# The opening of a fused light-convolution and max-of-three feed-forward kernel: how its weights arrive and are split, how the first tap sums are turned, and the order of its first steps

## The chip, the cores and the metric

One core of one Trainium2 chip runs the whole program. The metric is the device time of one execution in microseconds (us), the median of several runs. The profile is one more execution, recorded by the hardware.

## The reference, cut to what matters

```python
w = exp(weight_gen - max over the 7 taps); w = w / (sum over the 7 taps + 1e-9)   # (8, 4160, 8 heads, 7)
x_unf = x_pad[:, arange(S)[:, None] + arange(7)[None, :]]                         # the 7 last tokens
a = einsum('bshk,bskhg->bshg', w, x_unf)          # causal light convolution -> 33280 tokens x 192
h = maximum(maximum(a @ w1, a @ w2), a @ w3)      # w1, w2, w3: 192 x 768
out = h @ w_out                                   # w_out: 768 x 192
```

`x` and `weight_gen` are float32. The four weight matrices are float64, so each weight comes in as two 32-bit words.

## The kernel before

The 33280 tokens are cut into 65 chunks of 512 (`CH`), four token tiles of 128 each (`TC`). For a chunk, `taps` makes one product per tile (7 taps side by side, 1344 columns, line 492) on GpSimd or VectorE and sums it over the taps (line 504 on VectorE). The sum is turned so that its 192 features lie on the partitions: 128 of them in one tile (`xa`), the last 64 (`DB`) in another (`xc`). `up` multiplies by the differences w2-w1 and w3-w1 and takes maxima with zero; the part of w1 goes through a 192x192 matrix w1 @ w_out that `compose` builds once. `down` multiplies by w_out. So that the result is exact enough, every operand is a rounded high part and a low rest (`xa_hi`, `xa_lo`; `wa_hi`, `wa_lo`; `xc`, `xb`; `wb_hi`, `wb_lo`), and products are taken high by high, high by low and low by high.

Each product uses 64 rows of the TensorE array: the lower half of the rows ("L") and the upper half ("U") work on different products at the same time, but never in one bank together (`products`, line 1081). A bank is begun by L, then SyncE passes the word on, then U finishes it. So U trails L by some products, and all instructions of both stand in one TensorE queue in a fixed order. There are 8 PSUM banks (`"bank": 8`). One group `up c, j` is two banks with 18 products, 9 on each half of the rows. The weights of the last 64 features (`wb`) are kept on both halves of the partitions; block j of 128 columns of the feed-forward layer has its low rest (`wb_lo`) on the half `odd` only. Before, `jp, odd = divmod(j, 2)`, so every second block has five products on L and four on U, the others four and five.

The order on each engine is made by the program itself: `Plan` holds tasks with a cost, a due time and the buffers that they hold, and lays them out by a list schedule. The order of the first two chunks (`c < ON_TENSOR`) and of all weight preparation is written out by hand in `OPENING` (line 271). The steps there: `load*` issue DMAs on SyncE; `softmax` s; `singles` turns float64 into float32 (`single`, line 723); `a`, `b` are the weight differences (by two products with the identity and its negative on TensorE, lines 855 and 861, or on GpSimd, line 840); `rests` the low rests (line 902 on VectorE or GpSimd); `warm` n runs n products of the identity with itself (line 800); `turn x` and `turn y` turn the token sums (lines 538, 545, 557, 558); `turn` j turns w1 (lines 1013, 1014); `parts` makes high and low tokens (lines 611 to 634); `up`, `compose`, `down` as above. Everything whole (all 128 rows) on TensorE waits for the last U product before it.

In `single`, before, ScalarE takes the absolute value of the high word (line 742), VectorE or GpSimd clamps it (line 759; or ScalarE by two more passes, line 752), VectorE shifts (766), puts in the sign (775) and the top bits of the low word (784). The six loads of the last 64 rows (`load_b`, line 699) bring pieces of 1 KB, each load to 64 partitions (192 KB).

Of the kernel before, what the change touches and what calls it, by code (L numbers as in the profile page):

```python
# [12 lines left out]
U32 = mybir.dt.uint32  # L13
AF = mybir.ActivationFunctionType
# [179 lines left out]
def lightconv_maxout_kernel(  # L194
# [44 lines left out]
    CLAMP_ON_POOL = (("a", 0, 0), ("a", 2, 1), ("b", 2), ("d", 0), ("d", 1), ("d", 2),)  # L239
    CLAMP_ON_SCALAR = (("a", 1, 0), ("a", 2, 0), ("b", 1),)  # L240
    LOAD_DUE = {
        ("s", 0): -57,
        ("a", 0): -65,
        ("b",): -36,
        ("s", 1): -44,
        ("a", 1): -21,
        ("a", 2): -54,
        ("d",): 4,
# [9 lines left out]
    for c in range(1, NC):  # L258
# [7 lines left out]
    F_MAX = float(np.array(0x47EFFFFF, np.uint32).view(np.float32))  # L266
    F_MIN = float(np.array(0x38000000, np.uint32).view(np.float32))
# [6 lines left out]
        ("singles", 2), ("singles down",), ("taps", 0), ("taps", 1), ("warm", 27), ("a", 0, 1, 2),  # L274
        ("a", 0, 0, 1), ("turn x", 0, 1), ("turn x", 0, 0), ("turn x", 0, 2), ("turn y", 0, 1),
        ("turn x", 0, 3), ("turn", 5), ("turn y", 0, 2), ("turn", 0), ("turn", 1), ("a", 2, 0, 2),
# [3 lines left out]
        ("rests", "b", 0), ("parts", 0), ("turn y", 1, 3), ("turn", 4), ("b", 2),  # L280
# [10 lines left out]
    wb_hi = const.tile([P, NJ, NI, P], F32R, name="wb_hi")  # L291
# [28 lines left out]
        "bhi": ([P, NI, P], F32R),  # L320
# [5 lines left out]
        "bhi": 2, "raw": 1,  # L326
# [53 lines left out]
    def load_super(s):  # L380
# [14 lines left out]
        w = transfer(0.07 * n, weights, (), due, [hw])  # L395
# [127 lines left out]
    def turn_tokens(c, t):  # L523

        ha, sums = tapped[c]
        got, ba, bb = turned[c]
        to = slice(t * P, (t + 1) * P)

        if (c, t) in SUMS_ON_TENSOR:
            p, hr = sums[t]  # L530

            hb, hs = hold("bank"), hold("ob")

            def total():

                for k in range(K):
                    pin(
                        nc.tensor.matmul(
                            buf(hb)[:, :D], ident, buf(hr)[:, k], start=k == 0, stop=k == K - 1
                        )  # L540
                    )

            summed = whole(2.35, total, [p], [hb, hr])
            out = plan.add(
                "ACT", act(D), lambda: pin(nc.scalar.copy(buf(hs), buf(hb)[:, :D])), [summed],
                None, [hb, hs],
            )
            later["x", c, t] = [(hs, out)]
            return
        turn_sum(c, t, sums[t], lambda: buf(ha)[:, t], ha)  # L550
# [15 lines left out]
    def opening_parts(c):  # L566
        for t in range(TC):
            turn_later(c, t)
# [758 lines left out]
```

## Time and profile before

| | |
|---|---|
| median of 3 runs | 1409.42 us (1407.21 to 1411.99) |
| the profiled execution | 1407.7 us, of which its span is 1405.9 us |
| TensorE matmul busy | 1395.5 us, 99% of the span |
| VectorE, ScalarE, GpSimd busy | 72%, 80%, 78% |
| first product of an `up` | 36.0 us into the span |

Start by asking when the main products begin and whether they ever stop after that; then look at each engine in the stage before they begin. The busy share of TensorE counts pipelined products and also the identity products of `warm`, so it is no measure of progress in the opening.

### The profile page before, as it was taken

The page shows a single profiled execution, that of the slowest core. Times are in us where ns is not written, and L with a number is a line of the kernel's source. Part 1 is how long each engine was busy: PE and PEld are TensorE (multiplying, and loading weights), DVE is VectorE, ACT ScalarE, POOL GpSimd, SP SyncE. Part 2 cuts the span into 40 slices and gives each one's busy share as a digit, 9 for nine tenths or more (in the row PEclk, how much of TensorE's full clock was granted, in tenths as well). Part 3 has the DMA queues.
Part 4 walks back from the last instruction along what each step waited for, and adds up shares of the span by engine and source line. Part 5 has one row for each costly group of instructions (what it writes and reads, how often), then busy time and mean ns, then how long its engine had stood idle before and what let it go on. Part 6 is the DMA issues. An engine that isn't in the chain of part 4 may idle for free.

```text
span 1405.9 us, 37245 instructions
## 1 busy us (share of the span) xinstructions
PE 1395.5 (99%) x15000; PEld 1325.8 (94%) x15000; DVE 1009.6 (72%) x1378; ACT 1124.5 (80%) x2871; POOL 1095.1 (78%) x604
## 2 busy tenths in 40 slices
PE   8999999999999999999999999999999999999999
PEld 6999999999999999999999999999999999999998
DVE  7978777676687677677677677668668767767543
ACT  5787888887887787788788788788788778778873
POOL 6999898877887877887787788787788787788321
PEclk9999999999999999999999999999999999999999
DMA  7121111110111111111111011111011111110000
GB/s 257 47 70 70 59 70 70 59 70 24 59 70 69 59 70 37 57 59 69 70 58 63 31 59 69 70 59 69 24 59 70 70 59 70 35 55 15 24 24 23
DMA packets 23004, 85.10 MB, mean 61 GB/s; under 512 B 2488, under 2 KB 9144, under 8 KB 18864
## 3 DMA queue, kind: packets, MB, share of 16 engines
q1 hardware_dynamic: 22832, 82.73, 16.1%
q8 instruction: 117, 1.92, 0.6%
q14 instruction: 55, 0.45, 0.1%
HBM read 57.16 MB, written 25.56 MB: 59 GB/s over the span
## 4 chain that ended last, share of the span: by engine, by line
PE 98%; DMA 1%; SPq 0%; ACT 0%; DVE 0%; issue 0%
PE bank L1091 97%; DMA h_lo<-in_moe_w_dram 1%; DMA room<-in_moe_w_out_dram 0%; PE bank L1031 0%; SPq L683 0%; PE bank L861 0%; PE bank L855 0%; SPq L385 0%; PE bank L1014 0%; ACT xc L616 0%; PE bank L1013 0%; DVE bank L775 0%; PE bank L557 0%; SPq L390 0%; ACT wb_hi L967 0%
## 5 line engine op out<-in xcount | busy, mean ns | idle before, releaser
L492 POOL TENSOR_TENSOR r<-xt,wt 128x1344 f32<-128x1344 f32 x257 | 720.1, 2859 | 153.8 <-DVE acc L504 151.2
L1091 PE MATMUL bank<-wo,h_hi 64*128 64x384 f32 x3120 | 659.6, 355 | 0.0
L1091 PE MATMUL bank<-wo,h_lo 64*128 64x192 f32 x3120 | 593.2, 247 | 0.0
L1091 PE MATMUL bank<-xa_hi,wa_hi 64*128 64x512 f32 x1560 | 503.5, 389 | 0.0
L1091 PE MATMUL bank<-xa_lo,wa_hi 64*128 64x512 f32 x1560 | 500.2, 387 | 0.0
L1091 PE MATMUL bank<-xa_hi,wa_lo 64*128 64x512 f32 x1560 | 499.9, 387 | 0.0
L599 ACT COPY room<-room 32x128 f32<-32x128 f32 x1512 | 448.8, 297 | 63.7 <-DVE room L588 41.0
L1091 PEld LDWEIGHTS bank<-wo,h_lo 64*128 64x128 f32 x3120 | 486.2, 187 | 0.0
L1091 PEld LDWEIGHTS bank<-wo,h_hi 64*128 64x128 f32 x3120 | 482.6, 185 | 0.0
L504 DVE TENSOR_REDUCE acc<-r 128x192 f32<-128x1344 f32 x256 | 394.6, 1541 | 6.1 <-POOL r L492 5.6
L1091 PE MATMUL bank<-xc,wb_hi 64*128 64x512 f32 x780 | 293.4, 386 | 0.0
L1091 PE MATMUL bank<-xb,wb_hi 64*128 64x512 f32 x780 | 279.2, 387 | 0.0
L1091 PE MATMUL bank<-xc,wb_lo 64*128 64x512 f32 x780 | 278.4, 386 | 0.0
L1091 PEld LDWEIGHTS bank<-xa_lo,wa_hi 64*128 64x128 f32 x1560 | 265.6, 184 | 13.4
L1091 PEld LDWEIGHTS bank<-xa_hi,wa_lo 64*128 64x128 f32 x1560 | 265.2, 184 | 13.4 <-POOL wa_lo L902 0.2
L1148 ACT ACTIVATE m<-bank 128x512 f32<-128x512 f32 x390 | 233.1, 598 | 52.3 <-PE bank L1091 45.7
L1091 PEld LDWEIGHTS bank<-xa_hi,wa_hi 64*128 64x128 f32 x1560 | 262.2, 184 | 12.2 <-DVE acc L504 0.3
L1224 DVE TENSOR_TENSOR o<-bank,ob 128x192 f32<-128x192 f32 x260 | 90.4, 348 | 229.8 <-ACT ob L1217 229.8
L1167 DVE TENSOR_TENSOR h_lo<-bank,h_hi 128x512 fp32r<-128x512 f32 x258 | 176.4, 684 | 69.1 <-ACT h_hi L1160 68.9
L1167 POOL TENSOR_TENSOR h_lo<-m,h_hi 128x512 fp32r<-128x512 f32 x132 | 174.3, 1321 | 41.8 <-ACT h_hi L1160 41.7
L1156 DVE TENSOR_TENSOR bank<-bank,m 128x512 f32<-128x512 f32 x258 | 177.3, 688 | 19.1 <-ACT m L1148 9.0
L1091 PE MATMUL bank<-wca,xa_hi 64*128 64x384 f32 x520 | 182.7, 352 | 0.0
(104 smaller groups left out, 2043.0 us busy)
## 6 DMA issues: line engine op xcount, KB each, us to landing
xt<-in_x_dram SPq DMA_DIRECT2D x31, 1344.0 KB, 5.9
out_dram<-o SPq DMA_DIRECT2D x64, 384.0 KB, 2.3
wt<-in_weight_gen_dram SPq DMA_DIRECT2D x32, 224.0 KB, 2.5
h_hi<-in_moe_w_dram SPq DMA_DIRECT2D x6, 256.0 KB, 4.6
h_lo<-in_moe_w_dram SPq DMA_DIRECT2D x6, 192.0 KB, 9.8
xt<-in_x_dram SPq DMA_DIRECT2D x1, 960.0 KB, 6.2
raw<-in_moe_w_dram SPq DMA_DIRECT2D x3, 256.0 KB, 6.5
room<-in_moe_w_out_dram SPq DMA_DIRECT2D x2, 384.0 KB, 6.4
```

What stands on the lines that cost most here:

```text
L492: on.tensor_tensor(to, buf(hx)[:, la + t : la + t + K].rearrange("p k (h g) -> p k h g", g=G), wide() .rearrange("p (h k) -> p k h", k=K) ...
L504: pin(nc.vector.tensor_reduce(buf(ha)[:, t], buf(hr), axis=AX.X, op=ALU.add))
L599: pin(nc.scalar.copy(to[:, :, p : p + 32], b[p : p + 32, :, f : f + 32]))
L1091: ins = nc.tensor.matmul(buf(hb)[:, :n], w()[h], v()[h], start=half == 0 and first, stop=half == 1 and last,)
L1148: lambda: pin(nc.scalar.activation(buf(hm), buf(hb), AF.Relu)), [made], due,
L1156: lambda: pin(nc.vector.tensor_tensor(buf(keep), buf(hb), buf(hm), op=ALU.max)),
L1167: eng.tensor_tensor(buf(hl)[:, j], buf(keep), buf(hh)[:, j].bitcast(F32), op=ALU.subtract)
L1224: nc.vector.tensor_tensor(buf(ho)[:, t], buf(hb)[:, :D], buf(hq), op=ALU.add)
```

## The change

The edits, all in the opening but for the last but one:

1. `load_b` reads 3 KB pieces: three neighbouring blocks for one half of the partitions. So `odd, jp = divmod(j, 3)`: blocks 0 to 2 have their own `wb` rows on the lower half, 3 to 5 on the upper half.
2. In the first two chunks `up` uses these rows on their own half alone: the own half makes six products of a bank, the other three. Copies for the other half (`wb_of`) are made after the opening by two ScalarE copies (`change_over`); before, 12 copies (line 967) made both halves at once. For that, the rest of the last 64 features (`xb`) is made on both halves in these chunks.
3. `single`: ScalarE takes the scaled absolute value and, in a second pass over 16-bit words, the top bits of the low word; one minimum on VectorE or GpSimd; two VectorE operations put all together. The ScalarE clamp and the shift of line 766 are gone.
4. The tap sums on TensorE are made by seven transposes that add up in the bank, for each of the two feature parts, straight where they are wanted; before, seven identity products, a ScalarE copy (545) and a transpose. Five tiles instead of four do so; VectorE makes four products instead of three in the opening, all four in the contiguous layout.
5. All `a` and `b` differences and all rests but that of `b` 0 are on GpSimd.
6. `compose` makes its products on the two halves of the rows, without waiting for U.
7. In all chunks, blocks 0 to 2 now have five products on L and four on U, blocks 3 to 5 four and five.
8. `OPENING` is anew: no `warm`, `up 0 0` after c 0's sums and two tiles of c 1; `compose` after three groups instead of eight. Fewer low parts on GpSimd in these chunks (`ON_POOL_FIRST`), new due times of loads (their sequence is as before).

```diff
-    SUMS_ON_TENSOR = ((0, 1), (0, 2), (0, 3), (1, 2),)
+    SUMS_ON_TENSOR = ((0, 0), (0, 1), (0, 3), (1, 0), (1, 1),)
-    ON_POOL_FIRST = (1, 3, 4)
-    TAPS_ON_VECTOR = ((0, 1), (0, 3), (1, 1))
+    ON_POOL_FIRST = (5,)
+    TAPS_ON_VECTOR = ((0, 0), (0, 3), (1, 0), (1, 1))
...
-        ("a", 0): ("L", "DVE"),
+        ("a", 0): ("POOL", "POOL"),
         ("a", 1): ("POOL", "POOL"),
-        ("a", 2): ("L", "DVE"),
-        ("b", 0): ("POOL", "POOL"),
+        ("a", 2): ("POOL", "POOL"),
+        ("b", 0): ("POOL", "L"),
...
+        ("load down",), ("softmax", 0), ("softmax", 1), ("singles", 0), ("singles", 1),
+        ("singles", 2), ("singles down",), ("taps", 0), ("taps", 1), ("turn x", 0, 0),
+        ("turn x", 0, 2), ("a", 0, 1, 2), ("b", 1), ("turn x", 0, 3), ("rests", "b", 1),
+        ("turn x", 0, 1), ("parts", 0), ("turn x", 1, 0), ("b", 2), ("turn x", 1, 1), ("b", 0),
+        ("a", 2, 0, 2), ("turn", 5), ("a", 0, 0, 1), ("up", 0, 0), ("turn", 3), ("turn", 0),
+        ("rests", "b", 0), ("turn x", 1, 2), ("a", 1, 0, 2), ("turn x", 1, 3), ("turn", 4),
+        ("rests", "a", 1), ("turn", 2), ("parts", 1), ("rests", "a", 2), ("turn", 1),
+        ("rests", "a", 0), ("up", 0, 4), ("rests", "b", 2), ("up", 0, 3), ("compose",),
+        ("up", 0, 1), ("up", 0, 2), ("up", 0, 5), ("up", 1, 0), ("up", 1, 5), ("up", 1, 1),
+        ("down", 0), ("up", 1, 4), ("up", 1, 2), ("up", 1, 3),
...
+                for out, f in places():
+                    for k in range(K):
+                        pin(
+                            nc.tensor.matmul(
+                                out, buf(hr)[:, k, f], ident, is_transpose=True, start=k == 0,
+                                stop=k == K - 1,
+                            )
+                        )
...
-                                out=raw_b()[h, :, i].rearrange("p j n w -> p j (n w)"),
-                                in_=w[P:].rearrange("p (j o n) -> p j o n", j=NP, o=2)[:, :, odd],
+                                out=raw_b()[h, i].rearrange("p j n w -> p (j n w)"),
+                                in_=w[P:, odd * NP * 2 * P : (odd + 1) * NP * 2 * P],
...
+                nc.scalar.activation(big(), high().bitcast(F32), AF.Abs, scale=2.0**-112)
+                    fit(), big(), F_MAX, None, op0=ALU.min
+                    word(), source().bitcast(U16)[..., 1], AF.Copy, scale=2.0**-13, bias=-0.4999
...
+            own = half == odd
+            w, by = (wb_hi, [b_hi[jb]]) if own else (wb_of, b_of)
+            if c < ON_TENSOR:
+                got[2:2] = [of_k, of_b] if own else []
+            else:
+                got[2:2] = [of_b if half == low else of_k]
```

## Rows read from the trace of the kernel before

**Rows 1.** Part 4 of the page, by line: the chain of work that ended last, as shares of the span.

```profile
PE bank L1091 97%; DMA h_lo<-in_moe_w_dram 1%; DMA room<-in_moe_w_out_dram 0%; PE bank L1031 0%; SPq L683 0%; PE bank L861 0%; PE bank L855 0%; SPq L385 0%; PE bank L1014 0%; ACT xc L616 0%; PE bank L1013 0%; DVE bank L775 0%; PE bank L557 0%; SPq L390 0%; ACT wb_hi L967 0%
```

**Rows 2.** Busy time by stage: us of the stretch, then busy us (and instructions) of TensorE, its weight loads, VectorE, ScalarE, GpSimd, then TensorE's granted clock, the DMA share and GB/s.

```profile
0.00:36.00 36.00, 29.04 (x157) 24.76 (x157) 27.96 (x44) 19.63 (x50) 22.95 (x24) 0.95 0.76 251
36.00:58.70 22.70, 22.70 (x170) 19.94 (x170) 22.25 (x36) 16.18 (x35) 21.32 (x18) 1.00 0.00 1
...
200.00:400.00 200.00, 200.00 (x2184) 189.34 (x2181) 149.44 (x200) 166.54 (x428) 163.21 (x88) 1.00 0.16 60
```

**Rows 3.** TensorE in order of time, where the first `up` begins and around `compose` (start, us, what). The second row is the first product of U; the two at 54 us are the last of U before `compose`.

```profile
35.99 0.47 PE L1091 MATMUL bank<-xa_hi,wa_hi 64*128 64x512 f32 x1
...
37.48 0.50 PE L1091 MATMUL bank<-xa_hi,wa_hi 64*128 64x512 f32 x1
...
53.91 0.39 PE L1091 MATMUL bank<-xc,wb_hi 64*128 64x512 f32 x1
54.14 0.39 PE L1091 MATMUL bank<-xa_hi,wa_lo 64*128 64x512 f32 x1
54.45 4.31 PE L1031 MATMUL bank<-wo,raw 128*128 128x192 f32 x24
58.70 0.49 PE L1091 MATMUL bank<-xa_hi,wa_hi 64*128 64x512 f32 x1
```

**Rows 4.** The chain of work that ended last, in order of time (start, us, what): one of its pieces ahead of the first `up`, TensorE's products for a difference.

```profile
28.42 1.72 PE bank L861 x4
```

**Rows 5.** Two stretches of the loading, columns as in rows 2, then the packets of two stretches. In 14 to 16 us nearly all are pieces of the 64-partition loads of line 699; in 21.5 to 23.5 us they are pieces of w_out and the last of line 683, to 128 partitions.

```profile
15.00:18.00 3.00, 1.52 (x9) 0.96 (x7) 3.00 (x5) 0.46 (x2) 1.83 (x1) 1.00 1.13 237
...
24.00:27.00 3.00, 1.76 (x9) 1.13 (x10) 3.00 (x5) 2.06 (x7) 3.00 (x3) 1.00 1.07 422
...
DMA packets 447, 0.44 MB, mean 220 GB/s; under 512 B 37, under 2 KB 445, under 8 KB 445
...
DMA packets 512, 0.75 MB, mean 374 GB/s; under 512 B 29, under 2 KB 499, under 8 KB 512
```

**Rows 6.** The float64 split of the last 64 rows and what follows it, in order of time over all engines.

```profile
20.84 0.56 ACT L742 ACTIVATE m<-h_lo 128x384 f32<-128x384 f32 x1 [3.40 <-DMA h_lo<-in_moe_w_dram]
...
24.17 1.01 DVE L784 SCALAR_TENSOR_TENSOR b<-h_lo,bank 128x384 uint32<-128x384 uint32 x2
...
27.00 1.42 POOL L840 TENSOR_TENSOR b<-b 128x256 f32<-128x256 f32 x2
...
27.76 0.41 ACT L949 CAST bhi<-b 128x256 fp32r<-128x256 f32 x1 [0.50 <-POOL b L840]
...
28.38 0.73 POOL L902 TENSOR_TENSOR wb_lo<-b,bhi 128x256 fp32r<-128x256 f32 x1
...
32.12 0.55 DVE L784 SCALAR_TENSOR_TENSOR b<-h_lo,bank 128x384 uint32<-128x384 uint32 x1
```

**Rows 7.** TensorE in order of time: products of `warm` in two short stretches (the first and the second row), the first of eight transposes in a row and the products behind them, then two transposes at 30 us and two at 35 us.

```profile
4.72 1.49 PE L800 MATMUL bank<-ident 128*128 128x128 f32 x6
...
7.79 1.39 PE L800 MATMUL bank<-ident 128*128 128x128 f32 x11
...
25.23 0.33 PE L1013 MATMUL bank<-ident,w1a 128*128 128x128 f32 x1 [1.41 <-DVE b L784]
...
26.86 1.56 PE L855 MATMUL bank<-wx,ident 128*128 128x512 f32 x2
...
29.92 0.42 PE L557 MATMUL bank<-ident,ob 128*128 128x128 f32 x1
30.13 0.42 PE L558 MATMUL bank<-ident,ob 128*64 128x128 f32 x1
...
34.80 0.27 PE L557 MATMUL bank<-ident,acc 128*128 128x128 f32 x1
34.91 0.27 PE L558 MATMUL bank<-ident,acc 128*64 128x128 f32 x1
```

**Rows 8.** The stretch in which TensorE's granted clock was down, columns as in rows 2.

```profile
27.65:31.07 3.42, 3.42 (x10) 2.38 (x10) 3.42 (x6) 2.53 (x6) 2.03 (x4) 0.54 0.14 60
```

**Rows 9.** VectorE in order of time: two tap products in the contiguous layout, and one in the other.

```profile
11.94 3.02 DVE L492 TENSOR_TENSOR r<-xt,bank 128x1344 f32<-128x1344 f32 x2
...
25.57 2.62 DVE L492 TENSOR_TENSOR r<-xt,bank 128x1344 f32<-128x1344 f32 x1
```

**Rows 10.** Groups by line and shape in the first 57 us, of GpSimd and VectorE: count, busy us, mean ns, idle before.

```profile
L492 POOL TENSOR_TENSOR r<-xt,wt 128x1344 f32<-128x1344 f32 x9 | 23.8, 2672 | 3.9 <-PE bank L538 2.4 <-DVE acc L504 1.4
...
L840 POOL TENSOR_TENSOR b<-b 128x256 f32<-128x256 f32 x3 | 2.1, 731 | 0.0
...
L840 POOL TENSOR_TENSOR wx<-wx,w1a 128x512 f32<-128x512 f32 x1 | 1.3, 1287 | 0.0
...
L766 DVE TENSOR_SCALAR bank<-m 128x384 uint32<-128x384 uint32 x4 | 2.1, 548 | 0.0
```

**Rows 11.** TensorE at 311 us: L begins the first `down` of a chunk, and then U the same one.

```profile
311.12 0.33 PE L1091 MATMUL bank<-wca,xa_hi 64*128 64x384 f32 x1
...
313.89 0.33 PE L1091 MATMUL bank<-wca,xa_hi 64*128 64x384 f32 x1
```

**Rows 12.** VectorE at 311 us: the maximum of a block in its bank, and the last reader of that bank.

```profile
311.63 0.69 DVE L1156 TENSOR_TENSOR bank<-bank,m 128x512 f32<-128x512 f32 x1
...
313.45 0.68 DVE L1167 TENSOR_TENSOR h_lo<-bank,h_hi 128x512 fp32r<-128x512 f32 x1
```

More of the change, by code (lines that the diff above doesn't have):

```diff
@@ L527, in turn_tokens @@
         to = slice(t * P, (t + 1) * P)
+        both = c in LAST_ON_TENSOR
+        places = lambda: [
+            (buf(ba)[:, to], slice(0, P)),
+            *([(buf(bb)[:, to], slice(DB, D))] if both else []),
+            (buf(bb)[:DB, to], slice(P, D)),
+        ]
         if (c, t) in SUMS_ON_TENSOR:
             p, hr = sums[t]
[L532 to L539, printed above, removed]
-                        )
-                    )
@@ L543, in turn_tokens @@
[L543 to L548, printed above, removed]
-            return
-        turn_sum(c, t, sums[t], lambda: buf(ha)[:, t], ha)
-    def turn_sum(c, t, made_by, acc, held):
-        got, ba, bb = turned[c]
-        to = slice(t * P, (t + 1) * P)
-        def turn():
-            pin(nc.tensor.transpose(buf(ba)[:, to], acc()[:, :P], ident))
-            pin(nc.tensor.transpose(buf(bb)[:DB, to], acc()[:, P:], ident))
-        got.append(whole(0.36, turn, [made_by], [ba, bb, held]))
@@ L562, in turn_later, with turn @@
-    def turn_later(c, t):
-        for hs, out in later.pop(("x", c, t), ()):
-            turn_sum(c, t, out, lambda: buf(hs), hs)
-    def opening_parts(c):
-        for t in range(TC):
-            turn_later(c, t)
-        got, ba, bb = turned[c]
-        parts(c, [ba, bb], lambda: (buf(ba), buf(bb)[:DB]), got)
+            def turn():
+                for out, f in places():
[5 more added lines that the diff above has]
+                            )
+                        )
@@ L572, in blocks, with turn, opening_parts @@
+            got.append(whole((2.45 if both else 1.65), turn, [p], [ba, bb, hr]))
+            return
+        def turn():
+            for out, f in places():
+                pin(nc.tensor.transpose(out, buf(ha)[:, t, f], ident))
+        got.append(whole(0.47 if both else 0.36, turn, [sums[t]], [ba, bb, ha]))
+    def opening_parts(c):
+        got, ba, bb = turned[c]
+        parts(c, [ba, bb], lambda: (buf(ba), buf(bb) if c in LAST_ON_TENSOR else buf(bb)[:DB]), got)
     def blocks(c, ha, sums):
@@ L618, in parts @@
             )
-            for h in halves
+            for h in to_k
         ]
         for t in cs:
-            t.apart = True
-        name, cost = ("DVE", vec(CH)) if c < ON_TENSOR else ("POOL", gps(CH))
-        eng = nc.vector if c < ON_TENSOR else nc.gpsimd
-        near = halves[0] if c < ON_TENSOR else halves[low]
+            t.apart = len(cs) > 1
+        name, cost = ("DVE", vec(CH)) if first else ("POOL", gps(CH))
+        eng = nc.vector if first else nc.gpsimd
         def a_low():
@@ L1021, in turn_weights, with u_last, after, products @@
         )
+    SLOT = {CH: (0.2275, 0.386), 2 * D: (0.166, 0.358), D: (0.12, 0.247), "c": (0.335, 0.46)}
+    uppers = []
+    last_upper = []
+    def u_last():
+        return last_upper[-1:]
+    def after(ins, other):
+        tc.add_manual_dep(
+            ins.ins,
+            other.ins.name,
+            mybir.DependencyInfo(mybir.DependencyClass.Sync, mybir.DependencyReason.DATA),
+            reason="the two halves of the rows don't write to a bank together",
+        )
+        return ins
+    def products(hb, terms_of, to=None):
+        begun, before, at = {}, [], clock[0]
+        for half in range(2):
+            h = halves[half]
+            terms = terms_of(half)
+            for q, (n, w, v, deps, holds) in enumerate(terms):
+                first, last = q == 0, q == len(terms) - 1
+                def emit(n=n, w=w, v=v, h=h, half=half, first=first, last=last):
+                    ins = nc.tensor.matmul(
+                        to() if to else buf(hb)[:, :n], w()[h], v()[h],
+                        start=half == 0 and first, stop=half == 1 and last,
+                    )
+                    pin(ins)
+                    if half == 0 and last:
+                        begun[0] = pin(after(nc.sync.nop(), ins))
+                    elif half == 1 and first:
+                        after(ins, begun[0])
+                slot, end = SLOT[n]
+                t = plan.add(
+                    "LU"[half], slot, emit, [*deps, *(before if first else [])], at,
+                    [hb, *holds], end=end,
+                )
+                at += slot
+            if half == 0:
+                before = [plan.add("SYNC", 0.0, lambda: None, [t], None, [], end=0.3)]
+            else:
+                last_upper.append(t)
+        return t
     def compose():
```

219 lines of the change are left out of this document (82 added, 137 removed), and 7 rows, old and new, of the table OPENING.

## The prediction

> **What bounds the kernel now.** I read the chain of work that ended last first: the products of line 1091 hold 97% of it [rows 1]. Busy time by stage comes next: from 36 us on TensorE has no idle time and its granted clock is 1.00 [rows 2]. So the time is the moment when the first `up` begins (35.99), plus the products, plus whatever keeps one half of the rows waiting. The reader is to see two such losses in the order of time [rows 3]. U begins 1.49 us after L. And ahead of `compose` L has ended while U goes on: from 35.99 to 58.70 are 22.71 us for eight groups and `compose` (4.25). A product's slot is 0.23 [rows 3]; I use 0.228, so a half's nine slots of a group are 2.05 us and eight groups 16.4. 22.71 - 16.4 - 4.25 leaves 2.06 us lost. The chain ahead of 36 us goes through TensorE's products for a difference [rows 4]; VectorE is busy 27.96 of the first 36 us and 22.25 of the next 22.7 [rows 2], so it is nearly a second bound there.
>
> **Part by part.**
>
> **3 KB pieces.** While the 64-partition loads run, the DMA engines are busy all the time and move 237 GB/s; with 1.5 KB pieces to 128 partitions it is 374, with large ones 422 [rows 5]. The six loads are 1.18 MB: 5.0 us at 237, 3.15 at 374. The gain is 0 to 1.8 us, on the last landing that ScalarE waits for at 20.84 [rows 6]. The rows don't say whether the piece or the 64 partitions limit; 1.5 KB is only half as long again and runs 1.6 times as fast, which a fixed price per piece would hardly give. I take 0 and keep 1.8. The Trainium skill, SBUF — State Buffer, section "Door 1: The DMA port swizzle", speaks against this edit: a transfer to 64 partitions reaches only half of the ports, about 218 GB/s, and two such transfers at once are hardly faster. The trace's 237 agrees; by that rule longer pieces save nothing.
>
> **The split of b.** Before, the three parts are ready at 24.7, 25.2 and 32.7 [rows 6], the last one late by VectorE's queue. New: two ScalarE passes and two VectorE operations of 0.55 for the first part, as the rows of such operations show (0.56 at line 742 [rows 6], 0.548 at line 766 [rows 10]); the minimum is beside the second pass. 20.84 + 4 x 0.55 = 23.0, the others some 1.1 apart. The new 16-bit pass is not in the trace; 0.4 to 0.7 by line 742, 0.55 taken. Then the GpSimd difference (0.73 [rows 10]), ScalarE's copy (0.41 [rows 6]), and on TensorE the rest (768 columns in all, at two records of 0.11 for 128 columns of a plain product [rows 7], 1.3): 25.8 with three hand-overs of 0.1. GpSimd may be in a tap product of 2.67 [rows 10]: half of it on average, so the first `up` begins at 27.1. The other tap sums don't hold it at the full clock: five of 14 transposes at 0.11 [rows 7] are 7.7 us from about 11.6 (the first VectorE product begins at 11.94 now [rows 9] and can begin some 1.9 us earlier, as VectorE has less ahead of it, and takes 1.5).
>
> **From the first `up` to compose.** Group 0,0 has 6 slots on L and 3 on U per bank. L needs 12 slots, and U ends 3 later: 15 x 0.228 = 3.4 us before anything whole may run. Then come five `turn`s (0.41 each: four such pairs stand between 25.23 and 26.86 [rows 7]) and two token turns (0.22 and the gap, 0.36): 2.8 us. Group 0,4 takes 6 slots of L, 1.4. So group 0,3 begins 7.6 us after the first, and its place is 34.7 at the full clock.
>
> **The clock.** After the sums of c 1, TensorE waits for b, as it did at 25 us now. There it had a wait of 1.41 us and eight transposes in a row from 25.23 to 26.86, and the granted clock then was 0.54 in 27.65 to 31.07 [rows 7, 8]. At the 1.2 GHz level a transpose takes 0.21 instead of 0.11 [rows 7]. I expect one such fall around the first `up` and price it by this stretch: 3.4 us in which half the work is done, 1.7 lost. Group 0,3: 36.4, `compose` 1.4 later.
>
> **VectorE and GpSimd to that point.** VectorE: the 30 operations of the split have 11520 columns, 16.4 us at 0.548 for 384 [rows 10]; softmax 2.9, four tap products of 1.5 [rows 9] 6.2 (the third of before took 2.62 in the other layout), three sums 4.6, low parts of c 0 2.1, two groups' maxima and low parts 2.7: 34.9, less 0.09 for each of 48 operations, as neighbours overlap by that much: 30.6 from 4.2. With the 3.6 us of idle time that it has now that is 38.4, against `compose` at 37.8: the two engines meet. GpSimd: four products of 2.67 are 10.7, three `b` and two `a` differences of 0.73 and two of 1.29 are 6.2, and rests of the same lengths 4.8 [rows 6, 10]; softmax 2.5 and minima 2.0: 26.2 from 8.6, 34.8. So even a TensorE without waits would not get group 0,3 before about 34. The dropped identity products of `warm`, ScalarE's 12 copies of `wb` and VectorE's shift lie off this sum: they ran beside it. `change_over` (two ScalarE copies, about 0.75 each) is due 25 us later with ScalarE busy 83% [rows 2]: nothing; if it were late, all of U's products of c 2 wait behind it.
>
> **compose on halves.** 24 records of 4.31 us [rows 3] become 24 of 64 rows on each half, beside each other: the same 4.25. What it saves is the switch, up to the 2.06 us above; I take 2.0, bounds 0 and 2.06.
>
> **Blocks of five and four.** The L and U work of a chunk stays equal. But U trails L by 2.77 us at a chunk's `down`s now [rows 11], which is 12.2 slots; over blocks 3 to 5 L makes 24 products and U 30, so the trail grows to 18.2. At the end of the last chunk the trail is paid: 4 slots more than now, 0.9 us.
>
> **The sum.** By 36.4 L has done 18 slots, 4.1 us of work, which now is done at 35.99 + 4.1 = 40.1: 3.7 us gained. With the switch 2.0 and the trail -0.9: 4.8. The profiled execution's span 1405.9 becomes 1401.1, its own time 1407.7 becomes 1402.9; the median of the runs lies 1.7 above that execution, so 1404.6.
>
> **The rivals.**
>
> **A. Transposes leave the clock down.** Without `warm` TensorE has nothing but transposes until b's rest. In `warm`, plain products were spaced 0.23 at 5 us and 0.11 at 8 us [rows 7], so it starts at the low level. If transposes don't bring it up, each tap sum takes 14 x 0.21 = 2.9: five from 11.6, with a turn, `turn` 5 and the rest of b at half speed (0.4, 0.6, 2.6), end at 29.8. The first `up` loses 1.3 more. Group 0,3 at 38.8; gain 40.1 - 38.8 + 2.0 - 0.9 = 2.4: 1407.0. For: the clock fell behind eight transposes [rows 7, 8]. Against: these stood behind a wait, and were not dense. The Trainium skill, TensorE: Matmul & The Clock Gate, section "Part 4: PE-mode transpose", has this rule: transposes don't count as busy in the same way, and the full clock does not engage for them. The trace's fall agrees but doesn't prove it.
>
> **B. No fall, and b lands sooner.** The first `up` is at 25.3 or before; VectorE then sets `compose`, between 34.8 (no idle time) and 38.4, say 36.5. Group 0,3 at 35.1; gain 6.1, at best 8: 1403.3 to 1401.4. For: 1 KB pieces are the shortest here. Against: the 64 partitions stay.
>
> **C. Banks run out, in every chunk.** With a trail of 18.2 slots and four products to a bank of L, four and a half banks are begun by L and not ended by U, and L is in another; a block's bank is read until 2.5 us behind its maximum [rows 12], two or three more with the first of a pair: 7 to 8 of 8. Where L must wait for a bank, the trail can't grow and then shrink, and the chunk loses that slot on both halves: 0.228 x 63 = 14.4 us for one slot, 1404.6 + 14.4 = 1419. It decides from a third of a slot (4.8 us). Against: half of the blocks give their bank back at the maximum or earlier, and TensorE never waits for a bank now.
>
> **How the numbers follow.** Chances: forecast 0.40 (1402 to 1407.5, by the bounds of GpSimd's wait and of the fall, 0 to 3.4), A 0.30 (1405 to 1411), B 0.18, C 0.12. The range reaches from 1399 to 1412: it leaves out C and a tail of B. 0.3% of this kernel, about what a measurement tells from no change, is 4.2 us, that is 1405.2 below. Faster: B 0.18, half of the forecast 0.22, of A 0.03: 0.43. Slower: C and a tail of A: 0.13. Within: 0.44.
>
> **What would show it.** Right: first `up` near 27, a granted clock near 0.5 around it, `compose` near 38, no idle L ahead of it, 20.8 us a chunk as before. A: transposes of 0.21 up to 29 us. B: ScalarE's wait for b ending by 19.2. C: TensorE waiting for VectorE or ScalarE behind each block 5. Wrong altogether: a product or sum of c 0 late on VectorE or GpSimd, so that the in-order TensorE stands in front of it while others are ready.

## The result, and the profile after

Three rounds on one chip give a median of 1419.97 us for the changed kernel (1418.18 to 1424.81) beside 1409.01 for the kernel before: the ratio is 1.0085 [1.0064, 1.0105]. The change costs 11 us where 4.8 us of gain were forecast, and the time lies outside the range. The profiled execution took 1419.52 us with a span of 1417.6, against a span of 1405.9 before.

The chain that ended last, by line, of the changed kernel (it answers to [rows 1]): the line of the products has moved, and its share has fallen from 97% to 92%.

```profile
PE bank L1041 92%; POOL r L493 3%; DMA h_lo<-in_moe_w_dram 1%; DMA raw<-in_moe_w_dram 0%; POOL h_lo L1162 0%; POOL xb L628 0%; PE bank L544 0%; POOL xa_lo L623 0%; POOL wa_lo L892 0%; SPq L680 0%; POOL wt L457 0%; POOL wt L435 0%; POOL m L746 0%; ACT bank L756 0%; DVE r L493 0%
```

Busy time by stage, of the changed kernel (it answers to [rows 2], same columns and stretches):

```profile
0.00:36.00 36.00, 18.32 (x102) 15.08 (x102) 27.13 (x41) 18.82 (x44) 25.97 (x27) 0.95 0.74 251
36.00:58.70 22.70, 21.56 (x105) 14.36 (x105) 11.66 (x20) 11.26 (x25) 19.33 (x16) 0.85 0.00 1
200.00:400.00 200.00, 200.00 (x2199) 193.73 (x2197) 141.97 (x197) 162.70 (x421) 162.11 (x87) 1.00 0.15 55
```

The steady stage is as it was: TensorE never idle, granted clock 1.00, as many products. The stores of the output say the same: chunk 0's first store comes at 84.09 us (before 75.63), those of the next six chunks between 9.8 and 12.2 us later than before, and the very last 11.35 later. (In the new order nine groups stand ahead of the first `down` and not ten, so chunk 0's store would come about 2 us sooner even without a gain.) Nearly all that was lost was lost ahead of chunk 0's store. In the second row it can be seen: where TensorE made 170 records in 22.70 us, it makes 105, at a mean granted clock of 0.85, and VectorE is busy 11.66 in place of 22.25 us. TensorE counts as busy, and yet its weight loads have fallen from 19.94 to 14.36 us.

TensorE in order of time, of the changed kernel (it answers to [rows 3]: the first `up`, then what follows the turns, then the first record of `compose`, which now has line 1041):

```profile
31.23 0.50 PE L1041 MATMUL bank<-xa_hi,wa_hi 64*128 64x512 f32 x1
...
38.40 0.49 PE L1041 MATMUL bank<-xa_hi,wa_hi 64*128 64x512 f32 x1 [0.36 <-ACT raw L1010]
...
43.16 0.52 PE L1041 MATMUL bank<-wo,raw 64*128 64x192 f32 x1
```

The first `up` begins at 31.23: 4.76 us sooner than before, but 4.1 later than forecast. `compose` begins at 43.16 (forecast 37.8) and its last record ends at 61.11: 17.9 us for what was to be 4.25. That is where to look. Inside it, two stretches hold the second part of `compose` (64 features) and two do not; busy time by stage of the changed kernel, with the idle stretch ahead of the first `up` and the stretches of half clock beside them:

```profile
20.02:24.50 4.48, 0.01 (x1) 0.00 (x0) 2.98 (x5) 4.30 (x11) 3.71 (x3) 0.97 1.08 385
24.50:27.90 3.40, 3.28 (x17) 3.03 (x18) 3.40 (x6) 1.95 (x5) 2.67 (x3) 0.53 0.90 373
38.00:41.60 3.60, 2.46 (x14) 1.80 (x15) 2.38 (x6) 3.56 (x10) 3.60 (x5) 0.96 0.00 0
41.60:45.00 3.40, 3.40 (x20) 3.08 (x20) 1.61 (x3) 1.98 (x6) 3.40 (x3) 0.54 0.00 0
45.50:51.60 6.10, 6.10 (x26) 2.63 (x22) 2.01 (x3) 2.50 (x5) 5.46 (x5) 1.00 0.00 0
51.80:55.20 3.40, 3.40 (x21) 3.31 (x23) 1.84 (x3) 0.58 (x1) 1.47 (x2) 0.53 0.00 0
```

Read the last two rows against each other. From 45.50 to 51.60 the clock is at its full 2.4 GHz level and TensorE "busy", yet it makes 26 records in 6.10 us; from 51.80 to 55.20 it runs at 1.2 GHz and makes 21 in 3.40. The weight loads tell why: in the first they are busy 2.63 of 6.10 us, in the second 3.31 of 3.40. TensorE and its weight loads in order of time, in a piece of the first of these stretches:

```profile
47.11 0.54 PE L1041 MATMUL bank<-wo,raw 64*64 64x192 f32 x2
47.57 0.50 PE L1041 MATMUL bank<-xc,wb_lo 64*128 64x512 f32 x1
48.00 0.54 PE L1041 MATMUL bank<-wo,raw 64*64 64x192 f32 x2
48.47 0.50 PE L1041 MATMUL bank<-xa_hi,wa_hi 64*128 64x512 f32 x1
```

```profile
47.10 0.19 PEld L1041 LDWEIGHTS bank<-wo,raw 64*64 64x64 f32 x2 [0.36 <-issue]
47.57 0.18 PEld L1041 LDWEIGHTS bank<-xc,wb_lo 64*128 64x128 f32 x1 [0.28 <-issue]
48.00 0.19 PEld L1041 LDWEIGHTS bank<-wo,raw 64*64 64x64 f32 x2 [0.24 <-issue]
```

The two halves of the rows no longer work beside each other: two tiles of 64x64 for the one half (the two records that one float32 product of `compose` leaves), then a product for the other, each weight load beginning with the product that uses it and not under the one before. From tile pair to tile pair (47.11 to 48.00) are 0.89 us.

### The profile page after: what moved, and what is told of

Its sections match the earlier page's. It is cut to its first block, busy times and chain, and to the rows that moved or that the text cites. A ratio compares the mean times of both kernels' runs of the same rounds, so it can differ in the third digit from the quotient of the medians.

```text
span 1417.6 us, 37242 instructions
## 1 busy us (share of the span) xinstructions
PE 1394.8 (98%) x14962; PEld 1343.5 (95%) x14962; DVE 1001.7 (71%) x1372; ACT 1120.4 (79%) x2865; POOL 1105.0 (78%) x604
## 4 chain that ended last, share of the span: by engine, by line
PE 92%; POOL 5%; DMA 1%; issue 1%; ACT 0%; SPq 0%; DVE 0%; POOLq 0%; ACTq 0%
PE bank L1041 92%; POOL r L493 3%; DMA h_lo<-in_moe_w_dram 1%; DMA raw<-in_moe_w_dram 0%; POOL h_lo L1162 0%; POOL xb L628 0%; PE bank L544 0%; POOL xa_lo L623 0%; POOL wa_lo L892 0%; SPq L680 0%; POOL wt L457 0%; POOL wt L435 0%; POOL m L746 0%; ACT bank L756 0%; DVE r L493 0%
## 5 line engine op out<-in xcount | busy, mean ns | idle before, releaser
L1041 PE MATMUL bank<-xa_hi,wa_hi 64*128 64x512 f32 x1560 | 547.2, 390 | 0.5 <-ACT raw L1010 0.4
L1041 PE MATMUL bank<-xa_hi,wa_lo 64*128 64x512 f32 x1560 | 544.0, 388 | 0.8 <-POOL wa_lo L892 0.8
L1041 PE MATMUL bank<-xa_lo,wa_hi 64*128 64x512 f32 x1560 | 543.9, 387 | 0.0
L1041 PE MATMUL bank<-xc,wb_lo 64*128 64x512 f32 x780 | 297.8, 388 | 0.0
L1041 PEld LDWEIGHTS bank<-xa_hi,wa_hi 64*128 64x128 f32 x1560 | 273.9, 184 | 9.3 <-SPq L1047 0.5
L1041 PEld LDWEIGHTS bank<-xa_hi,wa_lo 64*128 64x128 f32 x1560 | 272.5, 184 | 9.9 <-POOL wa_lo L892 1.2
L1041 PEld LDWEIGHTS bank<-xa_lo,wa_hi 64*128 64x128 f32 x1560 | 272.8, 185 | 8.5 <-issue 0.3
L1162 POOL TENSOR_TENSOR h_lo<-m,h_hi 128x512 fp32r<-128x512 f32 x128 | 166.9, 1304 | 48.6 <-ACT h_hi L1155 47.6
L1151 DVE TENSOR_TENSOR bank<-bank,m 128x512 f32<-128x512 f32 x262 | 180.7, 690 | 23.5 <-PE bank L1041 13.7
L1212 ACT COPY ob<-bank 128x192 f32<-128x192 f32 x260 | 82.5, 317 | 107.8 <-PE bank L1041 100.5
L1155 ACT CAST h_hi<-bank 128x512 fp32r<-128x512 f32 x262 | 152.8, 584 | 16.2 <-DVE bank L1151 13.0
```

What stands on the lines that cost most here:

```text
L1041: ins = nc.tensor.matmul(to() if to else buf(hb)[:, :n], w()[h], v()[h], start=half == 0 and first, stop=half == 1 and last,)
L1151: lambda: pin(nc.vector.tensor_tensor(buf(keep), buf(hb), buf(hm), op=ALU.max)),
L1155: "ACT", act(CH), lambda: pin(nc.scalar.copy(buf(hh)[:, j], buf(keep))), [m], due + 1,
L1162: eng.tensor_tensor(buf(hl)[:, j], buf(keep), buf(hh)[:, j].bitcast(F32), op=ALU.subtract)
L1212: "ACT", act(D), lambda: pin(nc.scalar.copy(buf(hq), buf(hb)[:, D : 2 * D])), [made],
```

## The experiments

Eleven kernels ran, one of them twice. The theory was: **shape**, that is, a 64x64 product on one half does not run beside a 64x128 product on the other. Its rivals were the granted clock, the place of `compose` in the order, the queues ahead of the first `up`, and the loads.

**1. `compose` whole again, in the changed kernel**: `mult` makes a part's six products on all 128 rows, as in the kernel before.

```diff
-            got = products(hb, terms, lambda hb=hb, rows=rows: buf(hb)[rows, :D])
+            got = whole(2.1, mult, deps, [hb, hw1t])
```

> The changed kernel with compose made by 12 products over all 128 rows, as before, at the changed place in the order. Theory 1 (compose on halves is what costs: its 48 records and 36 products of up took 17.9 us in the changed kernel, for 8 us of work): compose takes 4.25 us plus about 2 for the switch, some 7 to 8 us less than now, so 1411 to 1414. Theory 2 (TensorE's order is starved by late tap products and GpSimd's minima, and compose only shows it): within 2 us of the changed kernel's 1420.

Measured: 1414.61, ratio to before 1.0050 [1.0033, 1.0067]; 5.4 of the 11 us are back. `compose` is one row of 4.31 us again, from 46.77. There is no stretch of half clock behind the first `up` any more. But the switch costs more here than the 2 us of theory 1. In the stretch ahead of `compose`, one half of the rows works alone, a product each 0.23 us:

```profile
42.60:46.77 4.17, 4.17 (x20) 3.12 (x17) 2.88 (x5) 3.94 (x8) 4.17 (x4) 1.00 0.00 0
```

**2. `compose` on halves alone, in the kernel before.** The reverse: before.py with only the lines of `compose` of the change.

> The kernel before with compose alone made on the two halves of the rows. Theory 1: 7 to 10 us slower than before, 1416 to 1419, with the same pattern of 64x64 products one after another with the products of up. Theory 2, and the prediction's step: 0 to 2 us faster than before, 1407 to 1409.

Measured: 1422.82, ratio 1.0106 [1.0087, 1.0126]: this one edit costs 14 us, more than the whole change and more than the 7 to 10 of theory 1. `compose` runs from 52.90 to 71.16, with the same turns, and the granted clock is 0.50 from 60 to 77 us.

**3. The second part 128 columns wide**, in the changed kernel: it computes features 64 to 191 in place of 128 to 191 (64 of them twice) and uses the upper 64. It is more work with the same number of records.

```diff
-        for n, (to, f) in enumerate(((wca, slice(0, P)), (wcb, slice(P, D)))):
+        for n, (to, f) in enumerate(((wca, slice(0, P)), (wcb, slice(DB, D)))):
-            hb, rows = hold("bank"), slice(0, f.stop - f.start)
+            hb, rows = hold("bank"), slice(0, P) if n == 0 else halves[1]
```

> The changed kernel, but compose's second part is made for 128 output columns (features 64 to 191, the last 64 are used) instead of 64, so that all products have the same 64x128 shape. Theory 1a (products of a 64x64 shape do not run beside products of a 64x128 shape on the other half): the serial stretches go, 6 to 9 us less, 1411 to 1414. Theory 1b (float32 products do not run beside rounded ones, whatever the shape): within 2 us of 1420. Theory 2: within 2 us of 1420.

Measured: 1409.68, ratio 1.0007 [0.9998, 1.0017]: 10.3 of the 11 us are back, by twice the work in the second part. The same kernel was run a second time, for its trace:

> The changed kernel with the second part of the composed product made 128 columns wide (features 64 to 191 in place of 128 to 191) on its own half of the rows, as in the run of that kind before, taken a second time for its trace. Theory (a 64x64 product on one half does not run beside a 64x128 or 64x512 product on the other, so part two went in turns): the records of part two begin inside the ends of the other half's products as those of part one do, 1409 to 1410.5 us again, compose and the products beside it over in 8 to 10 us where the changed kernel took 17.88, and chunk 0's store 9 to 11 us sooner than the changed kernel's 84.09. Rival (the wider part only lets the clock stay up): part two's records still go in turns, and the granted clock alone differs.

Measured: 1410.67, ratio 1.0011 [1.0001, 1.0020]. Busy time by stage and some rows of TensorE in order of time, of this kernel, from the first record of `compose` to just behind its last:

```profile
44.25:52.60 8.35, 8.35 (x90) 8.32 (x88) 6.51 (x10) 5.86 (x12) 8.35 (x6) 1.00 0.01 2
```

```profile
48.49 0.32 PE L1041 MATMUL bank<-wo,raw 64*128 64x192 f32 x1
48.61 0.39 PE L1041 MATMUL bank<-xc,wb_hi 64*128 64x512 f32 x1
48.65 0.48 PE L1041 MATMUL bank<-wo,raw 64*128 64x192 f32 x2
48.84 0.39 PE L1041 MATMUL bank<-xb,wb_hi 64*128 64x512 f32 x1
48.98 0.32 PE L1041 MATMUL bank<-wo,raw 64*128 64x192 f32 x1
```

90 records in 8.35 us, weight loads busy 8.32: the products of the one half start 0.16 apart and those of the other 0.23 apart, each as if it were alone. The chunk 0 store comes 9.16 us sooner than the changed kernel's. Shape is shown; the place in the order is not what cost. And at this place halves of one shape are 3.9 to 4.9 us faster than the whole `compose` of experiment 1, about the 4.2 us in which one half worked alone there.

**4. Size or place of the tile?** The changed kernel with its 64 features written to bank rows 64 to 127; nothing else moves, and the order of every engine is the same.

```diff
-            hb, rows = hold("bank"), slice(0, f.stop - f.start)
+            hb, rows = hold("bank"), slice(0, P) if n == 0 else halves[1]
```

> The changed kernel with the 64 features of the composed product's second part written to bank rows 64 to 127 in place of 0 to 63; the order of every engine and all sizes stay. Theory (it is the size, 64x64 beside 64x128, wherever the tile lies): part two still goes in turns with the other half's products, a weight load shown only once the product before it is over, some 0.45 us for each pair of tiles, and 1419 to 1421 us as the changed kernel. Rival (it is the place: both halves' tiles on the same columns as the first 64 of the other tile): the records lie beside each other as in the run with 128 columns, 1409 to 1411.

Measured: 1424.72 (1418.13 to 1425.29), ratio 1.0099 [1.0078, 1.0120]. The median lies 3.7 us above the range of the theory, for which no run here has the cause; the trace is that of the fastest of the four executions. TensorE in order of time, of this kernel:

```profile
46.18 0.49 PE L1041 MATMUL bank<-xc,wb_lo 64*128 64x512 f32 x1
46.60 0.54 PE L1041 MATMUL bank<-wo,raw 64*64 64x192 f32 x2
47.07 0.50 PE L1041 MATMUL bank<-xa_hi,wa_hi 64*128 64x512 f32 x1
47.40 0.39 PE L1041 MATMUL bank<-xa_lo,wa_hi 64*128 64x512 f32 x1
47.73 0.54 PE L1041 MATMUL bank<-wo,raw 64*64 64x192 f32 x2
```

The same turns: the size does it, not the columns on which the tile lies.

**5. Does `compose` on halves save the switch?** The kernel before with `compose` on halves, both parts 128 wide (the edits of 2 and 3).

> The kernel before, with the composed product alone made on half the rows, its second part 128 columns wide. By the prediction's step (4.25 us whole, 2.0 of switch saved): 1406.5 to 1409. By the theory of shapes (a part 64 wide cost the 14 us that the kernel before lost with the product on halves): those 14 come back, 1407 to 1410. Rival (the products on halves lose by the order or by the clock fall of 17 us that stood there): 1415 to 1423.

Measured: 1409.60, ratio 1.0005 [0.9996, 1.0015]. The 14 us are back, and nothing is gained in the end. On the spot the switch is saved: `compose` begins at 52.53 (before 54.45) on the half that is free first, and behind it L goes on at 56.29 (before 58.70) and U at 58.60 (before 60.03), where the first `up` was 0.4 us sooner. TensorE in order of time, of this kernel: L and U behind `compose`, L's first `down`, and a later product; then ScalarE's copy of the composed weights.

```profile
56.29 0.52 PE L1091 MATMUL bank<-xa_hi,wa_hi 64*128 64x512 f32 x1
58.60 0.52 PE L1091 MATMUL bank<-xa_hi,wa_hi 64*128 64x512 f32 x1
60.64 0.30 PE L1091 MATMUL bank<-wca,xa_lo 64*128 64x192 f32 x1
61.77 0.44 PE L1091 MATMUL bank<-wcb,xc 64*128 64x384 f32 x1
96.39 0.50 PE L1091 MATMUL bank<-xb,wb_hi 64*128 64x512 f32 x2 [0.61 <-POOL xb L634]
```

```profile
61.20 0.51 ACT L1059 CAST wcb<-wcb 64x384 fp32r<-64x384 f32 x1 [0.24 <-DVE wcb L1048]
```

Then the lead goes. L's first `down` stands for about 1 us until 61.77, as the copy of the composed weights begins at 61.20 (before 59.53), behind a VectorE step that stood in its queue until 60.81 (before 59.15). At 96.39 all of TensorE waits 0.61 us for `xb`. The last product of this execution comes 1.5 us later than that of the kernel before; not every piece of that loss is traced.

**6. The minimum on GpSimd.** The minima of the change turned out slower than the clamps with two operations that they replace. The kernel of 3, with the second operation given back:

```diff
-                    fit(), big(), F_MAX, None, op0=ALU.min
+                    fit(), big(), F_MAX, 0.0, op0=ALU.min, op1=ALU.max
```

> The same kernel, and the minimum on GpSimd given its second operation back (min, then max with 0.0, which changes no value). Theory (the form with one operation is what makes it slow, not what it reads or writes): 0.50 us for 384 columns and 0.61 for 512, as the clamp of the kernel before, where the changed kernel shows 1.15 to 1.18 and 1.31; the wait of 0.78 us for wa_lo gone, and the time 0 to 2 us less than the kernel with the wide part alone. Rival (the bank or the port is what slows it): 1.1 to 1.3 us still and the same time.

Groups by line and shape from 15 to 45 us (count, busy us, mean ns, idle before), first of the changed kernel, then of this one:

```profile
L746 POOL TENSOR_SCALAR m<-m 128x384 f32<-128x384 f32 x4 | 4.7, 1172 | 1.6 <-ACT m L739 1.6
...
L746 POOL TENSOR_SCALAR m<-m 128x512 f32<-128x512 f32 x1 | 1.5, 1494 | 0.0
...
L746 POOL TENSOR_SCALAR m<-m 128x256 f32<-128x256 f32 x1 | 0.9, 853 | 0.0
```

```profile
L746 POOL TENSOR_SCALAR m<-m 128x384 f32<-128x384 f32 x4 | 2.0, 511 | 2.5 <-ACT m L739 2.5
...
L746 POOL TENSOR_SCALAR m<-m 128x512 f32<-128x512 f32 x1 | 0.6, 615 | 0.0
L746 POOL TENSOR_SCALAR m<-m 128x256 f32<-128x256 f32 x1 | 0.4, 402 | 0.0
```

Less than half the time for one operation more. Measured: 1409.08, ratio 1.0002 [0.9992, 1.0012]; TensorE's wait of 0.78 us for `wa_lo` is gone. The median is 0.6 to 1.6 below the two runs of 3, which the intervals hardly tell from nothing.

**7. 1 KB pieces** in the changed kernel: each half's three pieces to a partition are fetched apart again, and lie block by block.

```diff
-        return raw(2)[:, : NP * RB].rearrange("p (i j n w) -> p i j n w", j=NP, i=3, w=2)
+        return raw(2)[:, : NP * RB].rearrange("p (j i n w) -> p i j n w", j=NP, i=3, w=2)
...
-                                out=raw_b()[h, i].rearrange("p j n w -> p (j n w)"),
-                                in_=w[P:, odd * NP * 2 * P : (odd + 1) * NP * 2 * P],
+                                out=raw_b()[h, i].rearrange("p j n w -> p j (n w)"),
+                                in_=w[P:, odd * NP * 2 * P : (odd + 1) * NP * 2 * P].rearrange("p (j n) -> p j n", j=NP),
```

> The changed kernel, with the last rows' words still in its layout on the chip but fetched in three pieces of 1 KB for each partition in place of one of 3 KB. If the run length carries b's landing: it lands 0.5 to 2 us later than 20.16, and the first product 0 to 2 us later than 31.23, 1420 to 1422. If it does not (768 packets of 23004 are all that changes): 20.2 to 20.8, and 1420 within 1 us.

Measured: 1419.19, ratio 1.0071 [1.0056, 1.0086]. ScalarE's first pass over b, of the changed kernel and of this one:

```profile
20.16 0.54 ACT L739 ACTIVATE m<-h_lo 128x384 f32<-128x384 f32 x1 [3.69 <-DMA h_lo<-in_moe_w_dram]
```

```profile
19.75 0.55 ACT L739 ACTIVATE m<-h_lo 128x384 f32<-128x384 f32 x1 [3.57 <-DMA h_lo<-in_moe_w_dram]
```

With three times as many pieces b lands no later. The prediction's value of 0 for the longer runs stands.

**8. The queue ahead of the first `up`.** In the changed kernel ScalarE's softmax copy of chunk 1 (line 476) stands behind the split of b, although its input was there at 19.14 (GpSimd's last softmax step begins at 18.17 and takes 0.97). ScalarE, VectorE and TensorE in order of time, one fence for each:

```profile
22.22 0.39 ACT L756 ACTIVATE bank<-h_hi 128x256 uint32<-128x256 uint16 x1
22.54 0.44 ACT L476 COPY bank<-wt 128x56 f32<-128x56 f32 x2
```

```profile
23.01 3.02 DVE L493 TENSOR_TENSOR r<-xt,bank 128x1344 f32<-128x1344 f32 x2
25.95 1.01 DVE L774 SCALAR_TENSOR_TENSOR b<-m,bank 128x384 uint32<-128x384 uint32 x2
```

```profile
24.62 4.75 PE L544 MATMUL bank<-ident,r 128*128 128x128 f32 x28 [4.60 <-DVE r L493]
```

So b's DMA holds ScalarE, ScalarE holds VectorE's tap products, these hold TensorE, which stands idle for 4.60 us, and b's own last step on VectorE waits behind the tap products until 25.95. With b's loads planned at 0.85 a piece instead of 0.51, the copy comes first; once in the changed kernel, once in the kernel of 6:

```diff
-                        0.51,
+                        0.85,
```

> The changed kernel, planned with a load of the last 64 rows at 0.85 us instead of 0.51 (the transfers themselves are the same). Theory of the queue: ScalarE's copies of c 1's softmax weights stood behind the split of b in its queue and so waited for b's landing at 20.1; planned later, they go ahead, c 1's two VectorE tap products begin by 20 instead of 23, and the first up begins 2 to 4 us earlier than 31.2; the time falls by as much, 1416 to 1418, or less where compose's loss hides it. Otherwise: first up at 31 and 1420.

Measured: 1428.16, ratio 1.0144 [1.0122, 1.0166]: 8 us worse, though the tap products begin at 19.59 and the first `up` at 29.63, 1.6 us sooner (2 to 4 were expected).

> The kernel with the 128-wide second part and the two-operation minimum, and b's loads planned at 0.85 a piece as in the kernel before (0.51 in the change), so that ScalarE's softmax copy of chunk 1 comes ahead of b's split. With b planned late in the changed kernel the first product came 1.6 us sooner and the time was 8 us worse. If that loss was the clock and the second part in turns: here first product 1 to 2 us sooner than in the kernel without it, and 1406.5 to 1409. If the other order itself loses: 1410 to 1418.

Measured: 1414.42, ratio 1.0037 [1.0023, 1.0051], in the range of the other order that loses by itself; the first `up` at 31.06 (31.37 in the kernel of 6), though b landed late in this execution (its split begins at 23.02, there at 19.49). Busy time by stage of the first and of the second kernel:

```profile
28.50:45.50 17.00, 16.91 (x55) 11.79 (x55) 12.32 (x21) 10.11 (x23) 15.38 (x14) 0.50 0.01 2
```

```profile
31.50:48.50 17.00, 16.91 (x58) 12.09 (x58) 12.54 (x20) 10.70 (x25) 13.16 (x14) 0.50 0.01 2
```

In both the half level, which the changed kernel had from 24.5 to 27.9 (mostly waits and transposes), falls on 17 us of products and turns. An earlier first `up` with a later fall is a loss. Expected was a gain; only the step on the queue was right.

**9. Fill the idle time.** The kernel of 6 with plain products of 128x128 on TensorE between the sums of chunk 0 and those of chunk 1; nothing else moves. First 32 of them, which left 64 records and took 7.31 us, then 17 (3.96 us).

```diff
-        ("turn x", 0, 1), ("parts", 0),
+        ("turn x", 0, 1), ("warm", 32), ("parts", 0),
```

> The kernel with the 128-wide second part and the two-operation minimum, and 32 plain products of 128x128 put on TensorE between the sums of chunk 0 and those of chunk 1, where it stands idle some 4.3 us; nothing else moves. Theory (the idle time ahead of 24 us is what lets the clock fall, which costs the sums of chunk 1 half their speed, 5.54 us where 28 at 0.11 to 0.12 are 3.3): granted clock 1.00 from 16 to 32 us, first product 1.5 to 2.2 us sooner, time 1 to 2 us less. Rival (VectorE and GpSimd set the compose anyway): first product sooner, compose where it was within 0.7 us, time the same within 0.7 us.

Measured: 1412.94, ratio 1.0030 [1.0020, 1.0040].

> The same kernel with 17 plain products where the run before had 32: those 32 left 64 records and took 7.31 us, longer than the idle time of 4.3 us that they were to fill, so that the sums of chunk 1 began 3.3 us late; 17 take 3.9 us. Theory A (the longer stretch of products was the fault): sums of chunk 1 from 24 us, 28 in some 3.2 us at the full clock, first product near 29.3 and 1405.5 to 1408.5. Theory B (a fall of the clock comes anyway in the stretch of turns and waits from 34 to 41 us, unless one has come before, and there it costs work on both halves): sums of chunk 1 at the full clock as in A, then a granted clock of 0.5 at some time between 32 and 47 us, 1410 to 1413.

Measured: 1410.31, ratio 1.0012 [1.0003, 1.0021]. Busy time by stage, first with 32, then with 17:

```profile
16.00:36.50 20.50, 19.45 (x148) 17.46 (x148) 14.47 (x21) 10.09 (x23) 13.52 (x12) 1.00 0.59 199
36.50:47.50 11.00, 10.48 (x41) 7.69 (x42) 8.46 (x16) 7.86 (x20) 10.93 (x12) 0.53 0.01 3
```

```profile
24.00:40.50 16.50, 13.18 (x81) 9.82 (x79) 15.94 (x24) 11.85 (x30) 14.21 (x15) 1.00 0.35 135
40.50:48.00 7.50, 7.27 (x33) 6.30 (x34) 4.31 (x8) 5.52 (x15) 7.43 (x8) 0.54 0.00 0
```

The fall ahead of the first `up` is gone, and another one comes later, on the products around `compose`. With 32 products the first `up` is at 31.77, no sooner than in the kernel of 6 (1.5 to 2.2 us sooner were expected): filling the idle time didn't remove the fall but moved it to where it costs. With 17 the median lies above theory A's range and inside B's. But the trace is that of the slowest of eleven executions, in which b's split began at 23.07 (19.49 in the kernel of 6) and the sums of chunk 1 at 27.61 instead of 24, so that TensorE still stood idle 2.20 us ahead of them. So B's later fall is shown for this execution, not for the faster ones. (By the medians the second kernel is 1.2 us slower than the kernel of 6, and their intervals overlap.)

## Why the prediction was wrong

What the profiled executions show together (single executions, those of 6 and 4 the fastest of their kernels; us; "half clock" is the time at the 1.2 GHz level behind the first `up`, and "in turns" says whether 64x64 tiles alternate with the other half's products):

| kernel | profiled execution | first `up` | `compose` | half clock | in turns |
|---|---|---|---|---|---|
| changed | 1419.52 | 31.23 | 43.16 to 61.11 | 6.8 | yes |
| 6: wide, two operations | 1407.04 | 31.37 | 41.01 to 48.91 | 0 | no |
| 9: the same, 32 products | 1412.94 | 31.77 | 46.47 to 54.79 | 10.2 | no |
| 8: the same, b planned late | 1415.07 | 31.06 | 47.28 to 55.85 | 17.1 | no |
| 4: other columns | 1418.13 | 32.16 | 42.44 to 59.71 | 3.4 | yes |

The lines of the table agree with two prices, both estimates from these lines. Half of the half-clock time is lost: 10.2 / 2 = 5.1 (5.9 measured from the second to the third line), 17.1 / 2 = 8.5 (8.0 to the fourth). And the turns cost 8.4: the two stretches 45.50 to 51.60 and 54.80 to 61.04 are 12.3 us, in which the 24 tiles, at the 0.163 of the wide ones, would need 2 x 12 x 0.163 = 3.9 beside the other half's work. For the changed kernel 8.4 + 6.8 / 2 = 11.8 of the 12.5 us between the first two lines; the rest is about the 0.78 us of the wait for `wa_lo`. For the last line it is 8.4 + 1.7 = 10.1 of 11.1. Two kernels outside the table: that of 1 lies 6.7 above the second line with neither, of which 4.2 are the switch and 0.9 the later first `up`; and the changed kernel with b planned late (1426.78) has 29.5 us of half clock behind its first `up` and the turns, 14.7 + 8.4 = 23.1 by these prices and 19.7 measured; some of its turns ran at the half clock, where the two prices count one loss twice.

By the prediction's steps:

- **The step that failed: "compose on halves ... beside each other: the same 4.25".** They didn't work beside each other, and `compose` took 17.9 us. The cost was read from a row of full-row products [rows 3] and carried over to 64x64 tiles, of which the trace of before had none beside 64x128 products; so the bound had to be open on the other side, and no rival had this mechanism. Widening the tiles alone gives back 9.3 to 10.3 us (experiment 3).
- **The switch, "I take 2.0, bounds 0 and 2.06"**, depends on what stands around it. At the changed place the whole `compose` leaves one half alone for 4.2 us, and halves of one shape win 3.9 to 4.9 us against it (experiments 1 and 3). In the order of before about 2 us of L and 1 of U are saved on the spot, and the time shows nothing of it (experiment 5).
- What a change of tile shape costs can be read off: a pair of tiles and one product need 2 x 0.163 + 0.23 = 0.56 us one after the other (an estimate, by the spacing of the wide tiles and of the products in experiment 3), and take 0.89. So the two changes of shape cost some 0.33 over and above the loss of working side by side. The Trainium skill, TensorEngine Tiling (Array Packing), section "Key Properties", has the rule that would have told it: changing the tiling mode, not just the tile, drains TensorE. The trace agrees, with these 0.33 us for two changes; the page gives no price.
- **The first `up` at 27.1**: mis-sized by 4.1 us. The sum had b's split, but not the in-order queue of ScalarE, through which b's landing also holds the tap products of chunk 1 (experiment 8); 1.6 of the 4.1 came back there, and the rest wasn't tried apart. In the kernel of 6, which has no turns, `compose` begins at 41.01, 3.2 later than forecast, and its profiled execution is 4.1 above the 1402.9 of the forecast. Counted without `compose`, its 160th product of line 1041 begins at 58.69, that of line 1091 before at 61.10: 2.4 us ahead, where the sum had 3.7 + 2.0 = 5.7 by then. The 3.3 that are missing are about the 3.2 by which `compose` is late, so the 2.0 for the switch is there. Behind that point another 1.3 us go, where the sum had 0.9 for the trail; the longest wait on TensorE's side is 0.54 us of a weight load for GpSimd's `xb` at 136 us.
- **The clock**: one fall around the first `up`, 3.4 us long, was forecast and came just ahead of it (24.50 to 27.90, granted 0.53). The two falls behind it were not, the first of them behind waits (TensorE busy 2.46 of 3.60 us), the second behind the turns. Rival A is false: the first 14 transposes took 3.22 us, 0.23 each, and 26 more that began at 16.62 took 3.40, 0.13 each, so transposes did bring the clock up. The Trainium skill, TensorE: Matmul & The Clock Gate, section "Part 4: PE-mode transpose", has it that the full clock doesn't engage for them; here the trace disagrees, since at 0.23 those 26 would have taken 6.0 us.
- **The minima "2.0 us"**: the six of line 746 between 20 and 40 us took 4.7 + 1.5 + 0.9 = 7.1; what was too little there is worth 0.6 to 1.6 us of the time (experiment 6).
- **Right**: the 3 KB pieces gain nothing (experiment 7), the steady stage stays (rival C false: the chunks' stores stay apart as before), and the trail is paid at the end: against the stores of the steady stage the last one comes 0.6 (kernel of 6) to 0.7 us (changed kernel) later still, where 0.9 was forecast.

No kernel here beats the kernel before by more than can be measured: the best, that of 6, is at 1.0002 [0.9992, 1.0012] with a first `up` 4.6 us sooner. Of these, five `turn`s (0.46 us each) and two token turns are only moved behind the first `up`. At the 160th product 2.4 us are left, at the last one 1.1; which of the other steps takes the rest was not tried.

## What to carry to other kernels

A TensorE that counts as 100% busy may be working on half of its rows: look at the number of records and at the weight loads' busy time in the same stretch, and at whether the starts of the two halves interleave. Before two streams share the array by halves, make every product of both of one tile shape, even at the price of columns that nobody reads: twice the work gave back 10 us here, and only then were halves faster than a product over all rows, where that would have left one half alone for 4 us. And a moment that comes earlier (first `up`: 1.6 us) or an idle time that is filled is no gain by itself where the granted clock may fall on the products behind it.

## What was not expected of the hardware

- 64x64 tiles on one half of the rows and 64x128 products on the other did not overlap in any trace here: 26 records in 6.10 us where 90 fit in 8.35 with one shape, whichever columns the tile lies on.
- On GpSimd the minimum with one operation takes 1.17 us for 128x384 (0.85 for 256 columns, 1.49 for 512), with a second operation behind it 0.51 (0.40, 0.62).
- A plain float32 product of 128x128 leaves two records of 0.114 us: 32 of them took 7.31 us.
- The same loads land up to 2 to 3 us apart from execution to execution: with an identical opening the first `up` began at 31.23 in the changed kernel and at 33.76 in the second run of experiment 3.
